# One conversion of the weights' low words: GpSimd in place of ScalarE

## The chip, the core and the metric

The program runs on one core of a Trainium2 chip. A core has five engines with a queue each: TensorE (PE for its matmuls, PEld for its weight loads), VectorE (DVE), ScalarE (ACT), GpSimd (POOL) and SyncE (SP), which here only issues DMAs. The metric is the device time of one execution in microseconds; lower is better.

## What is computed

Attention in a window for 8 batches and 8 heads (512 local and 32 global tokens, head size 64), followed by a feed-forward block over the 4352 resulting rows:

```python
s_ll = np.where(np.abs(pos[:, None] - pos[None, :]) <= 32, scale * q_l @ k_l.T, -1e9)
a_l = sm(np.concatenate([scale * q_l @ k_g.T, s_ll], axis=-1))
out_l = a_l @ np.concatenate([v_g, v_l])
out_g = sm(scale * q_g @ k_all.T) @ v_all
x = concat([out_g, out_l]) as rows of 512
h = x @ w_in                       # 512 x 2048
g = s * np.maximum(h, 0) ** 2 + b
out = g @ w_out                    # 2048 x 512
```

The two weight matrices come as float64. The kernel gets them as pairs of 32-bit words, a low word and a high word of each number, and makes float32 values of them on the chip.

## The kernel before

The attention is cut into 128 slots (`NS`), one for a batch, a half of its local tokens and a head. The feed-forward block works on 17 tiles of 256 rows, with 8 steps (`m`) of two 128-wide pieces of the hidden size each. One loop over `j` emits slot `j` of the attention, step `m = j - 10` of the feed-forward block, and the second product of the step before. In the first 16 slots the attention is computed on plain float32 operands (`scores32`, `transposes32`, `pv32`); from slot 16 on each operand is split into a rounded part and a rest (ScalarE rounds, GpSimd or VectorE subtracts: `split`, `v_split`, `g_load`). Between slots 0 and 9 blocks of four dummy matmuls (`keep_busy`) stand in TensorE's queue.

In those first 16 slots the weights are decoded too, one chunk of 128 hidden values in each: `weight_load` brings 512 KB of `w_in` and 512 KB of `w_out` into a staging tile `wst` (four buffers, whose places serve other tiles later), and `weight_words` decodes it in two halves of 128 x 512 numbers. So there are 32 halves. The six operations on a half, all in the functions printed below:

- line 160: the low words, every second word of `wst`, times 2^-29 as unsigned numbers, rounded into the integer tile `wup`. There are two places for `wup`, used in turn, so the one of a half can be written when the sum of line 165 two halves earlier has been read from it;
- line 161 (ScalarE): the high words as float, scaled, written over the low words of `wst`, thus only when line 160 has read them;
- line 164 (VectorE): those shifted left by three, in place;
- line 165 (VectorE): plus `wup`, an integer sum of two tiles in SBUF;
- line 168 (ScalarE): the rounded part into `w_all`;
- line 169 (VectorE): the rest into `w_all`. After this the staging buffer is free for the next load.

Each feed-forward step reads its two chunks of `w_all`, so the first tile of 256 rows can't be finished before the last chunk is decoded. The order of the instructions on each engine is set when the program is built, by a scheduler that plans with its own estimate of times; the loop's order and priorities enter it. Within an engine the instructions then run in that order.

Of the kernel before, what the change touches and what calls it, by code (L numbers as in the profile page):

```python
# [14 lines left out]
U32 = mybir.dt.uint32  # L15
U16 = mybir.dt.uint16
I16 = mybir.dt.int16
AF = mybir.ActivationFunctionType
ALU = mybir.AluOpType
# [46 lines left out]
def f32(ap):  # L66
    return ap.bitcast(F32)
# [3 lines left out]
def window_attention_then_ffn(ctx: ExitStack, tc: tile.TileContext, qd, qg, kw, vw, vg, qz, qgz, vz, w_in, w_out, sv, bv, out):  # L71
    nc = tc.nc
    scale = 1.0 / math.sqrt(D)
# [36 lines left out]
    for tile_, c0, shift in ((mask_low, 32, -32), (mask_mid, 32, 0), (mask_high, 0, 32)):  # L110
        nc.gpsimd.memset(tile_, 0.0)
        part = tile_[:, c0:c0 + 192]
        for sign, base in ((1, -shift), (-1, 64 + shift)):
            nc.gpsimd.affine_select(
                out=part, in_=part, pattern=[[sign, 192]], compare_op=ALU.is_ge,
# [31 lines left out]
    def weight_chunk(k):  # L147
        st = staged.pop(k)
        n = 2 if k < BY_HALVES else 1
        for i in range(n):  # L150
            c = 1024 // n
            weight_words(k, st[:, 2 * c * i:2 * c * (i + 1)], slice(c * i, c * (i + 1)))

    def weight_words(k, st, at):
        words = st.rearrange("p (n w) -> p n w", w=2)
        low, high = words[:, :, 0], words[:, :, 1]
        n = at.stop - at.start
        pool, tag = ((ops, "vsg"), (sb, "pg"))[(k + at.start // 512) % 2]
        up = pool.tile([P, n], I32, tag=tag, name=f"wup{k}_{at.start}", bufs=1)
        nc.scalar.activation(out=up, in_=low.bitcast(U32), func=AF.Copy, scale=2.0**-29)  # L160
        nc.scalar.activation(  # L161
            out=low.bitcast(F32), in_=high.bitcast(F32), func=AF.Prelu, scale=2.0**-112, alpha=2.0**32,
        )
        nc.vector.tensor_scalar(out=low, in0=low, scalar1=3, scalar2=None, op0=ALU.logical_shift_left)
        nc.vector.tensor_tensor(out=low, in0=low, in1=up, op=ALU.add)
        m = low.bitcast(F32)
        hi, lo = (w_all[:, i, k].rearrange("p w c -> p (w c)")[:, at] for i in range(2))
        nc.scalar.copy(out=hi, in_=m)  # L168
        nc.vector.tensor_sub(out=lo, in0=m, in1=f32(hi))  # L169
# [558 lines left out]
```

## Time and profile before

| | us |
|---|---|
| median of 3 runs (1012.46 to 1013.19) | 1012.96 |
| span of the profiled execution, first to last instruction | 1007.8 |
| TensorE matmul busy in the span | 993.5 |
| VectorE busy | 808.7 |
| ScalarE busy | 706.3 |
| GpSimd busy | 291.1 |

The median stands 5.2 us above the span of the profiled execution. Busy time of TensorE's matmuls runs to a modelled end, so the weight loads (904.7 us, 90% of the span) tell better where it stands still. All times in a trace are counted from the span's start.

### The profile page before, as it was taken

How to read it: one execution, taken by the hardware profiler on the slowest of the kernel's cores; microseconds unless marked ns; L12 is line 12 of the kernel's file. 1: busy time of each engine (PE TensorE's matmuls, PEld its weight loads, DVE VectorE, ACT ScalarE, POOL GpSimd, SP SyncE). 2: the span in 40 equal slices, each digit the busy share in tenths (PEclk: the TensorE clock that was granted, in tenths of full speed). 3: DMA queues.
4: the chain of work that ended last, by engine and by line, in shares of the span. 5: the costliest groups of instructions: out<-in, count | busy, mean ns of one | idle time of the engine just before them, and what ended most of it. 6: DMA issues, size and time to landing. Idle time of an engine off the chain costs nothing.

```text
span 1007.8 us, 20062 instructions
## 1 busy us (share of the span) xinstructions
PE 993.5 (99%) x6940; PEld 904.7 (90%) x6942; DVE 808.7 (80%) x2113; ACT 706.3 (70%) x1817; POOL 291.1 (29%) x366
## 2 busy tenths in 40 slices
PE   9899999999999999999999999999999999999998
PEld 5698899999999999999999999999999999999887
DVE  7999878978899779978799778988789788964322
ACT  8999867767677667858677667858677667743222
POOL 1001524323343233424243224424234223401000
PEclk9999999999999999999999999999999999999999
DMA  8765312213132212313122212313132112101000
GB/s 333 275 222 183 106 52 76 82 30 101 49 96 58 69 49 65 101 34 99 46 90 68 65 49 62 103 36 89 44 103 70 54 55 65 62 1 49 23 22 22
DMA packets 63845, 82.05 MB, mean 81 GB/s; under 512 B 7680, under 2 KB 51200, under 8 KB 63744
## 3 DMA queue, kind: packets, MB, share of 16 engines
q1 hardware_dynamic: 63168, 79.46, 25.4%
q10 hardware_dynamic: 576, 1.31, 0.4%
q8 instruction: 55, 0.90, 0.4%
q14 instruction: 46, 0.38, 0.1%
HBM read 71.30 MB, written 9.44 MB: 80 GB/s over the span
## 4 chain that ended last, share of the span: by engine, by line
PE 89%; ACT 7%; DVE 2%; DMA 1%; issue 0%; ACTq 0%; SPq 0%
PE ps_h L517 35%; PE acc L549 35%; PE ps_s L375 5%; PE ps_o L403 4%; PE turned L311 2%; PE turned L313 2%; PE ps_og L469 2%; ACT wst L161 1%; ACT w_all L168 1%; ACT wup L160 1%; PE ps_g L382 1%; ACT sm L231 1%; DMA wst<-in_w_out 1%; PE turned L447 1%; ACT pt L328 0%; DVE w_all L169 0%
## 5 line engine op out<-in xcount | busy, mean ns | idle before, releaser
L517 PE MATMUL ps_h<-xst,w_all 128*128 128x256 f32 x3264 | 437.0, 281 | 1.9 <-ACT xst L502 0.7
L549 PE MATMUL acc<-w_all,g 128*128 128x512 f32 x1632 | 421.5, 396 | 0.0
L517 PEld LDWEIGHTS ps_h<-xst,w_all 128*128 128x128 f32 x3264 | 406.9, 189 | 9.7 <-ACT xst L502 0.9
L549 PEld LDWEIGHTS acc<-w_all,g 128*128 128x128 f32 x1632 | 289.6, 188 | 49.7
L214 POOL TENSOR_TENSOR vs<-rv,vs 128x192 fp32r<-128x192 f32 x112 | 69.9, 624 | 313.3 <-ACT vs L213 312.2
L524 DVE SCALAR_TENSOR_TENSOR r<-ps_h,s_t,r 128x512 f32<-128x512 f32 x136 | 101.5, 746 | 52.4 <-ACT r L523 50.7
L231 ACT ACTIVATE sm<-sm,nm 128x224 f32<-128x224 f32 x256 | 121.7, 478 | 28.9 <-DVE nm L225 27.8
L532 DVE SCALAR_TENSOR_TENSOR g<-r,b_t,g 128x512 fp32r<-128x512 f32 x136 | 110.8, 815 | 35.6 <-ACT g L531 31.3
L531 ACT ACTIVATE g<-r,b_t 128x512 fp32r<-128x512 f32 x136 | 98.7, 725 | 52.2 <-DVE r L524 52.1
L206 POOL TENSOR_TENSOR kq<-rq,kq 128x256 fp32r<-128x256 f32 x112 | 94.5, 844 | 140.7 <-ACT kq L205 128.7
L523 ACT ACTIVATE r<-ps_h 128x512 f32<-128x512 f32 x136 | 81.3, 598 | 69.1 <-PE ps_h L517 58.1
L241 DVE TENSOR_SCALAR sm<-sm,nm 128x224 f32<-128x224 f32 x256 | 91.6, 399 | 3.9
L461 POOL TENSOR_TENSOR vsg<-rvg,vsg 128x320 fp32r<-128x320 f32 x64 | 57.1, 913 | 111.2 <-ACT vsg L460 111.2
L375 PE MATMUL ps_s<-kq 128*128 128x224 f32 x448 | 73.9, 275 | 1.9 <-DVE nm L225 1.9
L375 PEld LDWEIGHTS ps_s<-kq 128*128 128x128 f32 x448 | 67.2, 190 | 8.6 <-ACT kq L205 1.4
L392 ACT CAST pt<-turned 128x416 fp32r<-128x416 f32 x112 | 57.5, 513 | 24.8 <-PE turned L313 24.1
L393 DVE TENSOR_TENSOR pt<-turned,pt 128x416 fp32r<-128x416 f32 x112 | 65.5, 585 | 6.7 <-ACT pt L392 6.0
L386 ACT COPY tg<-ps_g 32x256 f32<-32x256 f32 (+1 forms) x112 | 42.1, 376 | 34.9 <-PE ps_g L382 32.5
L311 PE MATMUL turned<-ident,sm 128*96 128x128 f32 (+1 forms) x256 | 63.7, 273 | 1.2 <-ACT pt L328 1.0
L387 DVE TENSOR_TENSOR sg<-ps_g,tg 32x256 f32<-32x256 f32 (+1 forms) x112 | 48.2, 430 | 20.4 <-ACT tg L386 15.9
L204 POOL TENSOR_TENSOR kq<-rk,kq 64x352 fp32r<-64x352 f32 x56 | 61.7, 1102 | 4.4
L313 PE MATMUL turned<-ident,sm 128*128 128x128 f32 x256 | 62.8, 272 | 0.0
(81 smaller groups left out, 1288.7 us busy)
## 6 DMA issues: line engine op xcount, KB each, us to landing
rq<-in_qd SPq DMA_DIRECT2D x112, 128.0 KB, 2.1
rk<-in_kw SPq DMA_DIRECT2D x64, 176.0 KB, 2.3
rv<-in_vw SPq DMA_DIRECT2D x112, 96.0 KB, 1.9
rvg<-in_vg SPq DMA_DIRECT2D x32, 320.0 KB, 3.0
out<-o SPq DMA_DIRECT2D x32, 256.0 KB, 2.3
wst<-in_w_in SPq DMA_DIRECT2D x15, 512.0 KB, 4.6
wst<-in_w_out SPq DMA_DIRECT2D x15, 512.0 KB, 5.4
rv<-in_vz SPq DMA_DIRECT2D x16, 192.0 KB, 3.1
```

The source lines that it names most:

```text
L206: nc.gpsimd.tensor_sub(out=qs[:, 1, :], in0=rq, in1=f32(qs[:, 0, :]))
L231: nc.scalar.activation(out=p, in_=p, func=AF.Exp, bias=nm[:, blk:blk + 1], scale=-1.0, accum_out=ss[:, blk:blk + 1],)
L241: nc.vector.tensor_scalar(out=p, in0=p, scalar1=ss[:, blk:blk + 1], scalar2=1.0, op0=ALU.mult, op1=ALU.mult,)
L311: nc.tensor.transpose(out=p_t[0:n, s0:s0 + P], in_=sm[:, c0:c0 + n], identity=ident)
L313: nc.tensor.transpose(out=p_t[:, o0:o0 + P], in_=sm[:, c0:c0 + P], identity=ident)
L375: nc.tensor.matmul(p_s[:, W * blk:W * blk + W], lhsT=qs[:, a, blk * P:(blk + 1) * P], rhs=ks[:, KEYS[blk]], start=(a == 0), stop=(a == 1),)
L517: nc.tensor.matmul(p_h[:, k], lhsT=wi[:, a, f, c], rhs=xs[:, e, c, :], start=(n == 0), stop=(n == 11),)
L523: nc.scalar.activation(out=r, in_=p_h, func=AF.Relu)
L524: nc.vector.scalar_tensor_tensor(out=r, in0=p_h, scalar=s_t, in1=r, op0=ALU.mult, op1=ALU.mult)
L531: nc.scalar.activation(out=g[:, 0], in_=r, func=AF.Identity, bias=b_t)
L532: nc.vector.scalar_tensor_tensor(out=g[:, 1], in0=r, scalar=b_t, in1=f32(g[:, 0]), op0=ALU.add, op1=ALU.subtract,)
L549: nc.tensor.matmul(oacc[t][i], lhsT=g[:, a, k, i * P:(i + 1) * P], rhs=wo[:, e, f, :], start=(pr == 0 and n == 0), stop=(pr == 7 and n == 5),)
```

## The change

Line 160 is the only one that changes. The product with 2^-29 and the conversion from unsigned words to integers is issued to GpSimd as a tensor-scalar multiplication, no longer to ScalarE as an activation. Operands, tiles and buffers stay.

```diff
-        nc.scalar.activation(out=up, in_=low.bitcast(U32), func=AF.Copy, scale=2.0**-29)
+        nc.gpsimd.tensor_scalar(out=up, in0=low.bitcast(U32), scalar1=2.0**-29, scalar2=None, op0=ALU.mult)
```

The scheduler orders the program anew. On ScalarE the 32 instructions of line 160 leave the queue. At the second chunk (`wst_148`), before the change:

```order
L160 ACTIVATE wup_0_194<-wst_148 128x512
L300 COPY sg_176<-ps_g_313 64x256
L161 ACTIVATE wst_148<-wst_148 128x512
L160 ACTIVATE wup_512_201<-wst_148 128x512
L161 ACTIVATE wst_148<-wst_148 128x512
L328 COPY pt_233<-turned 128x416
L168 CAST w_all<-wst_148 128x512
```

and with it:

```order
L161 ACTIVATE wst_148<-wst_148 128x512
L328 COPY pt_233<-turned 128x416
L161 ACTIVATE wst_148<-wst_148 128x512
L168 CAST w_all<-wst_148 128x512
L231 ACTIVATE sm_315,nm_316<-sm_315,nm_316 128x224
L328 COPY pt_330<-turned 128x416
L231 ACTIVATE sm_315,nm_316<-sm_315,nm_316 128x224
L168 CAST w_all<-wst_148 128x512
```

Each line 161 now follows an instruction of another engine, where it followed one of its own queue.

On GpSimd the 32 instructions stand behind the making of the masks; most of them run where the queue held nothing, and the last ones among the first splits of queries, keys and values (`kq`, `vs`). The end of that stretch, as a difference (+ is with the change):

```order
+L160 TENSOR_SCALAR wup_512_919<-wst_729 128x512
 L214 TENSOR_TENSOR vs_1353<-rv_1198,vs_1353 128x3x64
+L160 TENSOR_SCALAR wup_0_912<-wst_729 128x512
+L160 TENSOR_SCALAR wup_0_1012<-wst_827 128x512
+L214 TENSOR_TENSOR vs_1475<-rv_1293,vs_1475 128x3x64
+L160 TENSOR_SCALAR wup_512_1019<-wst_827 128x512
+L160 TENSOR_SCALAR wup_512_1105<-wst_909 128x512
 L206 TENSOR_TENSOR kq_1091<-rq_1010,kq_1091 128x256
 L204 TENSOR_TENSOR kq_1091<-rk_1008,kq_1091 64x352
 L206 TENSOR_TENSOR kq_1091<-rq_1096,kq_1091 128x256
-L214 TENSOR_TENSOR vs_1475<-rv_1293,vs_1475 128x3x64
+L160 TENSOR_SCALAR wup_0_1098<-wst_909 128x512
```

All but the last conversion now stand ahead of the splits for slot 16 (`kq_1091`).

VectorE has the same instructions, in a somewhat other order. At the fourth chunk (`wst_191`), before the change:

```order
L164 TENSOR_SCALAR wst_191<-wst_191 128x512
L165 ISA wst_191<-wst_191,wup_0_291 128x512x2
L234 TENSOR_SCALAR nm_373<-nm_373 128x2
L164 TENSOR_SCALAR wst_191<-wst_191 128x512
L235 RECIPROCAL nm_373<-nm_373 128x2
L225 ISA sm_418,nm_419<-ps_s_413,mask_low 128x224
L225 ISA nm_419 128x1
L225 ISA sm_418,nm_419<-ps_s_413,mask_mid 128x224
L225 ISA nm_419 128x1
L165 ISA wst_191<-wst_191,wup_512_298 128x512x2
L241 TENSOR_SCALAR sm_372<-sm_372,nm_373 128x224 x2
```

and with it:

```order
L169 TENSOR_TENSOR w_all<-wst_151,w_all 128x512
L241 TENSOR_SCALAR sm_372<-sm_372,nm_373 128x224 x2
L169 TENSOR_TENSOR w_all<-wst_151,w_all 128x512
L234 TENSOR_SCALAR nm_419<-nm_419 128x2
L164 TENSOR_SCALAR wst_191<-wst_191 128x512
L235 RECIPROCAL nm_419<-nm_419 128x2
L165 ISA wst_191<-wst_191,wup_512_298 128x512x2
L241 TENSOR_SCALAR sm_418<-sm_418,nm_419 128x224 x2
L164 TENSOR_SCALAR wst_191<-wst_191 128x512
```

The softmax of the next slot (`sm_418`, `nm_419`) has moved ahead of the fourth chunk; what comes right behind line 165, whose end lets the next conversion into its `wup` tile, is in both orders mostly an instruction on tiles in SBUF (lines 234, 241, 164, 169).

## Rows read from the trace of the kernel before

**Rows 1.** The page: busy tenths in 40 equal slices of the span.

```profile
DVE  7999878978899779978799778988789788964322
ACT  8999867767677667858677667858677667743222
```

**Rows 2.** Busy by stretch: length, then PE, PEld, DVE, ACT, POOL (instructions), clock, DMA.

```profile
6.20:103.30 97.10, 90.90 (x563) 74.33 (x564) 92.60 (x265) 94.73 (x221) 7.03 (x8) 1.00 0.70 247
...
10.00:50.00 40.00, 35.21 (x201) 25.02 (x202) 37.76 (x132) 39.82 (x100) 0.00 (x0) 1.00 0.85 308
50.00:90.00 40.00, 40.00 (x274) 36.73 (x273) 38.15 (x99) 39.66 (x87) 1.03 (x1) 1.00 0.69 237
90.00:110.00 20.00, 17.37 (x111) 15.14 (x110) 18.49 (x45) 18.57 (x45) 10.02 (x12) 1.00 0.28 84
110.00:900.00 790.00, 790.00 (x5650) 731.51 (x5649) 674.46 (x1776) 569.83 (x1518) 271.57 (x333) 1.00 0.23 67
```

**Rows 3.** Chain of waits, 4 to 104 us: shares, and one piece (start, us, what).

```profile
by line: ACT wst L161 14.3%; ACT w_all L168 14.3%; ACT wup L160 14.1%; ACT sm L231 13.1%; DMA wst<-in_w_out 10.6%; ACT pt L328 4.4%; DVE w_all L169 3.9%; DVE wst L165 3.8%; DVE wst L164 2.7%; ACT g L531 2.5%; ACT r L523 2.4%; issue 2.2%; AC
...
22.89 0.57 ACT wup L160
```

**Rows 4.** Groups, 4.8 or 6.2 to 103.3 us: count | busy us, mean ns | idle before.

```profile
L160 ACT ACTIVATE wup<-wst 128x512 int32<-128x512 uint32 x32 | 22.2, 692 | 2.6 <-DMA wst<-in_w_in 2.2 <-DMA wst<-in_w_out 0.4
L161 ACT ACTIVATE wst<-wst 128x512 f32<-128x512 f32 x32 | 21.8, 685 | 0.2
...
L169 DVE TENSOR_TENSOR w_all<-wst,w_all 128x512 fp32r<-128x512 f32 x32 | 23.1, 723 | 0.8 <-ACT w_all L168 0.4
L165 DVE CUSTOM_DVE_ANT_0 wst<-wst,wup 128x1024 uint16<-128x1024 uint16 x32 | 22.4, 701 | 0.2
L164 DVE TENSOR_SCALAR wst<-wst 128x512 int32<-128x512 int32 x32 | 13.6, 424 | 7.0 <-ACT wst L161 6.7
```

**Rows 5.** Timeline of VectorE near 27 us: start, us, what.

```profile
26.59 0.69 DVE L165 CUSTOM_DVE_ANT_0 wst<-wst,wup 128x1024 uint16<-128x1024 uint16 x1
...
27.68 0.68 DVE L169 TENSOR_TENSOR w_all<-wst,w_all 128x512 fp32r<-128x512 f32 x1
```

**Rows 6.** Timeline of GpSimd, then of VectorE, 92 to 97 us.

```profile
92.30 0.96 POOL L206 TENSOR_TENSOR kq<-rq,kq 128x256 fp32r<-128x256 f32 x1
93.33 1.28 POOL L204 TENSOR_TENSOR kq<-rk,kq 64x352 fp32r<-64x352 f32 x1
94.69 1.07 POOL L206 TENSOR_TENSOR kq<-rq,kq 128x256 fp32r<-128x256 f32 x1
96.21 0.59 POOL L214 TENSOR_TENSOR vs<-rv,vs 128x192 fp32r<-128x192 f32 x1 [0.45 <-ACT vs L213]
...
92.68 1.12 DVE L165 CUSTOM_DVE_ANT_0 wst<-wst,wup 128x1024 uint16<-128x1024 uint16 x1
93.75 1.42 DVE L169 TENSOR_TENSOR w_all<-wst,w_all 128x512 fp32r<-128x512 f32 x1
95.09 0.74 DVE L524 SCALAR_TENSOR_TENSOR r<-ps_h,s_t,r 128x512 f32<-128x512 f32 x1
...
96.37 0.98 DVE L169 TENSOR_TENSOR w_all<-wst,w_all 128x512 fp32r<-128x512 f32 x1
```

**Rows 7.** GpSimd's instructions by line and shape, whole span: count | busy us, mean ns.

```profile
L214 POOL TENSOR_TENSOR vs<-rv,vs 128x192 fp32r<-128x192 f32 x112 | 69.9, 624 | 313.3 <-ACT vs L213 312.2 <-PE ps_s L375 1.1
...
L461 POOL TENSOR_TENSOR vsg<-rvg,vsg 128x320 fp32r<-128x320 f32 x64 | 57.1, 913 | 111.2 <-ACT vsg L460 111.2
...
L114 POOL TENSOR_SCALAR_AFFINE_SELECT mask_low<-mask_low 128x192 bf16<-128x192 bf16 x2 | 0.7, 345 | 0.0
...
masks.py:199 POOL TENSOR_SCALAR_AFFINE_SELECT ident<-ident 128x128 f32<-128x128 f32 x1 | 0.3, 292 | 0.0
```

**Rows 8.** The key splits on GpSimd by tile: shortest, median, longest ns.

```profile
L206 POOL TENSOR_TENSOR kq<-rq,kq x112: 724/740/1309, 92.3 to 872.5; 128x256 fp32r<-128x256 f32 x112
...
L204 POOL TENSOR_TENSOR kq<-rk,kq x56: 937/1109/1283, 93.3 to 871.3; 64x352 fp32r<-64x352 f32 x56
```

## The prediction

> **What bounds the kernel now.** I read the 40 slices of the page first [rows 1]. The four slices of the first 100 us look unlike the rest: ScalarE and VectorE both stand at eight or nine tenths. All that the change touches lies there: the weights are decoded between 4.8 and 103.3 us [rows 4]. The table by stretch says what each part is worth [rows 2]. From 110 to 900 us TensorE's weight loads are busy 731.5 of 790 us (93%) and nothing else is full: that part is TensorE's own. From 10 to 50 us they are busy 25.0 of 40 us (63%), from 50 to 90 us 36.7 of 40 (92%, as later), and from 90 to 110 us 15.1 of 20 (76%). So TensorE loses time in the first 110 us, by waiting for the engines that decode weights and do the softmax. A microsecond that this head gains or loses moves the end by a microsecond, because the work that TensorE has behind the last decoded chunk stays the same.
>
> Which engine sets the head? The chain of waits runs along ScalarE: line 160 alone has 14.1% of the 100 us from 4 to 104 [rows 3]. In the stretch from VectorE's first decoding step to the end of its last one, 6.2 to 103.3 us, ScalarE is busy 94.7 of 97.1 us; but VectorE is busy 92.6 of the same 97.1 [rows 2]. It is idle for 4.5 us in all. This is the number on which the case turns: the chain names ScalarE, and VectorE stands 4.5 us behind it.
>
> **What the change takes away.** ScalarE loses 32 instructions. A piece of line 160 takes 0.57 us of the chain [rows 3] (its 692 ns of [rows 4] overlap the neighbours), so 32 x 0.57 = 18.2 us leave ScalarE's queue. ScalarE would then need 94.7 - 18.2 = 76.5 us of the 97.1. VectorE's own work is not shortened by it at all: it still has 92.6 us to do. What can be won is its idle time, 4.5 us, and not all of that: some is the gap between one engine's end and the next one's start, and some a staging load still under way. I let 1.5 us of it stay: gain 3.0 us, bounds 0 and 4.5.
>
> **What it adds.** 32 instructions on GpSimd, whose queue was empty for most of this time (7.0 us busy of 97.1 [rows 2]). Its own time is covered many times over. A conversion can start when line 165 two halves earlier has ended; halves come every 97.1 / 32 = 3.0 us, so 6.1 us are there for the conversion, line 161 (0.69), line 164 (0.42) and what they queue for. On ScalarE, line 161 now waits for GpSimd, with exponentials and roundings of other slots queued behind it; ScalarE has 18 us to spare for that. The loads of `wst` stay on their queue and still wait for line 169. All of this I cost at nothing, as long as a conversion takes under 3 us or so.
>
> What is not covered is what GpSimd does to VectorE. Near 27 us, with GpSimd idle, line 165 takes 0.69 us and line 169 0.68 [rows 5]. Between 92.3 and 96.8 us GpSimd works on four splits, and in that time line 165 takes 1.12, one line 169 takes 1.42 and another 0.98 [rows 6]. Line 524, one of whose operands is in PSUM, takes 0.74 in the same time, as it always does. So an instruction of VectorE on two tiles in SBUF stands still while GpSimd is at work. The loss there is 0.43 + 0.74 + 0.30 = 1.47 us for four instructions of GpSimd, 0.37 us for one. It is the same mix of work on VectorE as in the rest of the head: lines 164, 165 and 169 alone are 59 of its 92.6 us [rows 2, 4].
>
> These four were 256, 352, 256 and 192 elements long; taken at the medians for the first three and the mean for the fourth (740, 1109, 740, 624 ns [rows 7, 8]) one is about 0.80 us. The trace has no conversion on GpSimd, so I bound it. From above, by its two-operand rows: 624 ns for 192 elements and 913 for 320 are 2.26 ns per element, which makes 913 + 192 x 2.26 = 1.35 us for 512 [rows 7]. From below, by its rows with one operand: 292 ns for 128 and 345 for 192 are 0.83 ns per element, so 345 + 320 x 0.83 = 0.61 us [rows 7]. The conversion reads one tile, which puts it nearer to the lower end, but also converts at either side of the product, which the mask rows don't. I take 0.80 us. The loss per instruction is then that of the four, 0.37 us, and 32 x 0.37 = 11.8 us. At 0.61 us a wait is shorter by 0.19: 32 x 0.18 = 5.8 us. At 1.35 us it is longer by 0.55: 32 x 0.92 = 29.4 us. That a conversion costs VectorE nothing can't be excluded by these rows, since all four splits read two tiles; the lowest end is therefore 0.
>
> The Trainium skill has a rule on that last point. Its page "SBUF — State Buffer", section "Who interferes with whom", says that GpSimd and VectorE share a pair of ports under an exclusive lock, and that a VectorE instruction with two SBUF inputs, or in a mode that uses both ports, contends with any GpSimd instruction that reads SBUF. By it one operand is enough and the sum stands at 11.8 us; without it the lower end would be 0. The rows of two-operand splits agree with it (1.12 us against 0.69 for line 165); that a one-operand instruction does the same, no row here shows.
>
> **The sum.** VectorE in the head: 92.6 + 11.8 us of work and waits and 1.5 us idle, 105.9 us where there were 97.1. That is 8.8 us more, and VectorE takes ScalarE's place as the bound. The span of 1007.8 becomes 1016.6; with the 5.2 us that the median stands above the span, 1021.8 us. With 5.8 to 18 us of loss the same case gives some 1015 to 1029 us.
>
> **The rivals.**
> - *The chain's promise.* The head gives back what line 160 has on the chain, 14.1 us [rows 3]: 1012.96 - 14.1 = 998.9 us. Against it stand VectorE's 4.5 idle us: it would have to finish 92.6 us of work in 83. It would take a head in which VectorE's rows hold slack inside.
> - *No contention with one operand.* If the conversion leaves VectorE alone, the freed ScalarE gives the idle time back: 3.0 us, 1010.0 us, and 1008.5 at most. This one ends on the faster side; it decides as soon as the loss per conversion is under 3.0 / 32 = 0.09 us. For it: no row shows a one-operand instruction beside a slowed VectorE. Against: splits of every line are seen to do it.
> - *A short conversion.* GpSimd runs at the pace of its one-operand rows, 0.61 us: 5.8 us lost and 3.0 to 4.5 won, 1014.3 to 1015.8 us. The page "GPSIMD Engine Reference" of the Trainium skill, section "Engine selection", speaks for it: one-input operations there run at roughly line rate. The mask rows (0.83 ns per element) agree; whether a conversion from strided words does, none shows.
> - *A long conversion.* At the two-operand rate or slower, 29.4 us lost and 3.0 won: 1039.4 us. For it: reading every second word and converting twice may cost GpSimd as much as a second operand.
>
> **How the numbers follow.** Forecast (VectorE bound, 1021.8): 0.58. Short conversion: 0.13. No contention: 0.12. Long conversion: 0.13. The chain's promise: 0.04. The runs of before spread over 0.7 us, and about 0.2% (2 us) is what a measurement can tell from no change. Faster by more: the chain's promise and most of no contention and a little of the short conversion, 0.15. Within: more than half of the short conversion and the rest of no contention, 0.12. Slower: 0.73. For 8 times in 10 the range has to take in the forecast's own 1015 to 1029, the short conversion, a part of no contention, and some of the way to the long one: 1010 to 1034.
>
> **What would show it.** In the head of the changed kernel: lines 165, 169 and 164 longer than their 0.69, 0.68 and 0.42 us wherever a line 160 of GpSimd lies beside them, by about 0.37 us for each line 160; the last line 169 ending near 112 us, not 103.3; VectorE full and ScalarE at about 75 to 80% up to there; TensorE's losses all before 120 us, and the same 93% after it; the chain of waits in the head on VectorE and GpSimd. I am wrong in size if line 160 takes far from 0.80 us on GpSimd; wrong in the mechanism if lines 165 and 169 keep their length beside it, or if the head ends earlier than 103 us although VectorE works as long as before.

## The result

The changed kernel takes 1024.59 us (median of 1021.07 to 1026.19) where the kernel before takes 1012.71 in the same comparison: a ratio of 1.0121, 95% interval [1.0106, 1.0136]. That is slower by 11.9 us, on the side the prediction named and inside its range, 2.8 us above its 1021.8.

The profiled execution took 1024.31 us, its span is 1022.5. The profiled execution of before, with its span of 1007.8, was about 3 us quicker than its own median: in all kernels run here the time of a profiled execution stands 1.8 to 2.2 us above its span, so it took some 1010. Differences between the two traces (14.7 us in the span) are therefore about 3 us larger than that of the medians.

The 40 slices of the page, to be held against [rows 1]: the first four of ScalarE stand at 6 to 8 tenths, no longer 8 or 9, VectorE's stay as full as they were, and TensorE's granted clock, 1.00 in every slice before, dips in the fourth and fifth.

```profile
DVE  6999888898799788998789788988899788964322
ACT  6876676777678676777678676867678676844222
PEclk9998899999999999999999999999999999999999
```

The table by stretch, to be held against [rows 2]; the first row runs from VectorE's first decoding step to the end of its last one. Columns: stretch and length, then busy time (instructions) of PE, PEld, DVE, ACT and POOL, granted clock, share of the DMA engines, GB/s.

```profile
7.30:115.70 108.40, 94.74 (x550) 76.66 (x549) 103.78 (x265) 80.14 (x191) 61.02 (x39) 0.94 0.66 222
...
10.00:50.00 40.00, 35.53 (x201) 24.96 (x200) 39.57 (x128) 32.97 (x86) 20.60 (x13) 1.00 0.85 293
50.00:90.00 40.00, 37.78 (x253) 34.68 (x253) 38.74 (x94) 29.11 (x66) 22.49 (x13) 1.00 0.63 207
90.00:110.00 20.00, 13.03 (x70) 10.70 (x68) 17.99 (x28) 13.45 (x27) 15.02 (x12) 0.82 0.43 139
110.00:130.00 20.00, 19.35 (x119) 17.34 (x120) 15.82 (x41) 14.34 (x39) 8.58 (x10) 0.84 0.24 66
130.00:900.00 770.00, 769.17 (x5498) 711.59 (x5498) 658.48 (x1738) 557.88 (x1490) 266.68 (x329) 1.00 0.23 68
```

VectorE issues the same 265 instructions in the head as before, but needs 103.78 us for them instead of 92.60, and the head is 108.4 us long instead of 97.1. It is idle for 4.6 us of it, before 4.5. ScalarE fell from 98% busy to 74%. TensorE's weight loads lose nothing of their busy time up to 50 us (24.96 against 25.02), 2.0 us from 50 to 90, 4.4 us from 90 to 110 and 1.4 us from 110 to 130; behind 130 us they are busy 92% of the time, as before.

Busy time hides a part of this. The kernel before has from 110 to 130 us:

```profile
110.00:130.00 20.00, 20.00 (x155) 18.75 (x154) 18.58 (x44) 16.27 (x45) 10.70 (x12) 1.00 0.34 101
```

The changed kernel is about as busy there, but with 119 matmuls at a granted clock of 0.84 in place of 155 at 1.00. Counted in matmuls it falls behind by 0, 21, 41 and 36 in the four stretches from 10 to 130 us, by 98 in all. At the 0.14 us that one takes behind 130 us (770 us for 5498) these are some 13.7 of the 14.7 us; this is an estimate, since the matmuls differ in size.

The groups of VectorE for the same stretch (line, tiles, shapes, count, then busy us, mean ns, then idle time before), to be held against [rows 4], and GpSimd's from the page of the whole execution:

```profile
L169 DVE TENSOR_TENSOR w_all<-wst,w_all 128x512 fp32r<-128x512 f32 x32 | 26.2, 823 | 1.2 <-ACT w_all L168 0.9
L165 DVE CUSTOM_DVE_ANT_0 wst<-wst,wup 128x1024 uint16<-128x1024 uint16 x32 | 22.4, 700 | 1.0
L164 DVE TENSOR_SCALAR wst<-wst 128x512 int32<-128x512 int32 x32 | 16.0, 504 | 7.4 <-ACT wst L161 7.2
L241 DVE TENSOR_SCALAR sm<-sm,nm 128x224 f32<-128x224 f32 x34 | 14.1, 455 | 0.1
...
L234 DVE TENSOR_SCALAR nm<-nm 128x2 f32<-128x2 f32 x17 | 5.0, 292 | 0.2 <-ACT sm L231 0.2
...
L160 POOL TENSOR_SCALAR wup<-wst 128x512 int32<-128x512 uint32 x32 | 55.7, 1741 | 38.7 <-DVE wst L165 20.3
```

Two of VectorE's groups are not in the rows shown of before; in the head there (6.2 to 103.3 us) they read:

```profile
L241 DVE TENSOR_SCALAR sm<-sm,nm 128x224 f32<-128x224 f32 x34 | 9.9, 331 | 0.1
...
L234 DVE TENSOR_SCALAR nm<-nm 128x2 f32<-128x2 f32 x17 | 3.2, 189 | 0.3
```

So at equal counts line 169 costs 3.1 us more, line 241 4.2, line 164 2.4, line 234 1.8; line 165 keeps its length. A conversion takes 1741 ns on GpSimd in the mean. How the two engines meet is seen in the timelines of GpSimd and of VectorE (start, us, what):

```profile
82.49 1.70 POOL L160 TENSOR_SCALAR wup<-wst 128x512 int32<-128x512 uint32 x1 [2.33 <-DVE nm L235]
84.37 1.90 POOL L160 TENSOR_SCALAR wup<-wst 128x512 int32<-128x512 uint32 x1 [0.18 <-DVE wst L165]
87.85 1.96 POOL L160 TENSOR_SCALAR wup<-wst 128x512 int32<-128x512 uint32 x1 [1.58 <-DVE wst L165]
...
83.61 0.68 DVE L165 CUSTOM_DVE_ANT_0 wst<-wst,wup 128x1024 uint16<-128x1024 uint16 x1
84.21 1.73 DVE L169 TENSOR_TENSOR w_all<-wst,w_all 128x512 fp32r<-128x512 f32 x2
...
88.35 0.86 DVE L164 TENSOR_SCALAR wst<-wst 128x512 int32<-128x512 int32 x1
89.13 0.68 DVE L169 TENSOR_TENSOR w_all<-wst,w_all 128x512 fp32r<-128x512 f32 x1
...
114.96 0.69 DVE L169 TENSOR_TENSOR w_all<-wst,w_all 128x512 fp32r<-128x512 f32 x1
```

At 88.35 line 164 takes 0.86 us instead of 0.42, and the line 169 behind it, still beside the same conversion, its usual 0.68. VectorE loses 0.44 us to a conversion that lasts 1.96. At 83.61 line 165 lies beside a conversion and keeps its 0.68 us.

The trace shows the same over the whole head. The table counts, for each line, the instructions that lie beside no instruction of GpSimd, those that lie beside conversions alone, and how many of either are lengthened (over 0.1 us longer than the shortest of the line); the other three of lines 164, 165 and 169 each lie beside splits.

| line | beside nothing: lengthened | beside conversions alone: lengthened |
|---|---|---|
| 241 | 11: 0 | 23: 12 |
| 234 | 11: 0 | 6: 6 |
| 164 | 15: 0 | 14: 5 |
| 169 | 8: 0 | 21: 7 |
| 165 | 19: 0 | 10: 0 |

So none of these instructions grew where GpSimd stood still, and not every meeting costs. What decides which one does isn't shown. The last line 169 ends at 115.65 us.

### The profile page after: what moved, and what is told of

It reads as the page before. It is cut to its first block, busy times and chain, and to the rows that moved or that the text cites. A ratio compares the mean times of both kernels' runs of the same rounds, so it can differ in the third digit from the quotient of the medians.

```text
span 1022.5 us, 20162 instructions
## 1 busy us (share of the span) xinstructions
PE 1000.9 (98%) x6942; PEld 909.1 (89%) x6942; DVE 819.8 (80%) x2113; ACT 690.8 (68%) x1785; POOL 345.5 (34%) x398
## 4 chain that ended last, share of the span: by engine, by line
PE 78%; DVE 1%; ACT 1%; DMA 0%; issue 0%; DVEq 0%; ACTq 0%
PE acc L549 31%; PE ps_h L517 31%; PE ps_s L375 4%; PE ps_o L403 4%; PE turned L311 2%; PE turned L313 2%; PE ps_og L469 2%; PE ps_g L382 1%; PE turned L447 1%; ACT sm L231 0%; DMA rq<-in_qd 0%; ACT kq L203 0%; DVE r L524 0%; DVE sm L241 0%; PE turned L500 0%
## 5 line engine op out<-in xcount | busy, mean ns | idle before, releaser
L549 PE MATMUL acc<-w_all,g 128*128 128x512 f32 x1632 | 426.8, 399 | 3.0 <-ACT g L531 3.0
L241 DVE TENSOR_SCALAR sm<-sm,nm 128x224 f32<-128x224 f32 x256 | 94.9, 412 | 4.0
L160 POOL TENSOR_SCALAR wup<-wst 128x512 int32<-128x512 uint32 x32 | 55.7, 1741 | 38.7 <-DVE wst L165 20.3
L403 PE MATMUL ps_o<-pt,vs 128*128 128x256 f32 x336 | 62.9, 295 | 0.0
```

What stands on the lines that cost most here:

```text
L241: nc.vector.tensor_scalar(out=p, in0=p, scalar1=ss[:, blk:blk + 1], scalar2=1.0, op0=ALU.mult, op1=ALU.mult,)
L403: nc.tensor.matmul(p_o[:, :, q], lhsT=vs[0:n, c], rhs=pt[0:n, :, o], start=(c == 0), stop=(c == 1))
L549: nc.tensor.matmul(oacc[t][i], lhsT=g[:, a, k, i * P:(i + 1) * P], rhs=wo[:, e, f, :], start=(pr == 0 and n == 0), stop=(pr == 7 and n == 5),)
```

## The experiments

Two questions stood open. Is the loss VectorE's meeting with GpSimd, or the new waits on GpSimd? And what part of it is the order, which the scheduler makes anew for every edit?

**No conversion at all (e1).** L165 adds a tile of zeros, so the low words' part is left out.

```diff
-        nc.scalar.activation(out=up, in_=low.bitcast(U32), func=AF.Copy, scale=2.0**-29)
+        up = no_up[:, 0:n]
```

> The kernel before with line 160 left out: nobody converts the low words, and line 165 adds a tile of zeros that is written once (so the lowest three bits of the weights are missing). ScalarE loses its 32 conversions, GpSimd gets nothing. Theory of VectorE as the bound: what can be won is VectorE's idle time in the head, 0 to 4.5 us, so 1008 to 1013 us. Rival, the chain names the bound: the 14 us that line 160 has on the chain come off, about 999 us.

Measured: 1019.6 us, ratio 1.0076 [1.006, 1.0093]. Less work on ScalarE, nothing on GpSimd, and still 8 us slower: both theories failed. The profiled execution was the slowest of the four, 1023.66 us. What TensorE waited for (line, releaser: us, times, longest), two stretches, and the lines 169 (shortest, median, longest ns, then first and last start):

```profile
PE ps_g L295 <- DMA rk<-in_kw: 6.3, 2, 3.6
```

```profile
40.00:50.00 10.00, 5.97 (x23) 4.22 (x24) 9.24 (x31) 6.95 (x17) 0.00 (x0) 0.77 0.80 277
60.00:70.00 10.00, 6.95 (x31) 6.08 (x32) 8.32 (x20) 8.23 (x18) 0.54 (x1) 0.66 0.69 216
```

```profile
L169 DVE TENSOR_TENSOR w_all<-wst,w_all x32: 668/687/695, 8.4 to 97.5; 128x512 fp32r<-128x512 f32 x32
```

The last chunk is decoded at 98.2 us, 5 us earlier than before; the time was lost elsewhere. In the new order key loads came late, TensorE stood, and its clock fell between 40 and 70 us, where the kernel before has 1.00. An order can thus cost most of what the change costs (7.7 us here, 11.9 there), and no kernel that is planned anew tells the price of its edit alone.

**The conversion beside the kernel before (e2).** ScalarE keeps its conversion; GpSimd makes a second one that nobody reads.

```diff
+        nc.gpsimd.tensor_scalar(out=low, in0=low.bitcast(U32), scalar1=2.0**-29, scalar2=None, op0=ALU.mult)
```

> The kernel before, with line 160 on ScalarE as it was, and a second conversion of the same shape on GpSimd behind line 169, whose result nobody reads (it goes over the words of the staging tile, which are dead by then). Nothing waits for it but the next load into the staging tile. Theory of the port: VectorE stands still for some 0.35 us per conversion, lines 164, 169 and 241 grow by some 11 us in sum, and the time is 1020 to 1026 us although ScalarE works as before. Rival, the waits for GpSimd's result make the difference: 1012 to 1014 us.

Measured: 1022.35 us, ratio 1.0108 [1.0093, 1.0123]. Nobody waits for the result, and the loss is there. But it isn't clean: the tile it writes is the staging tile, and the next weight load waits for it. SyncE's queue (line, releaser: us, times, longest):

```profile
SPq L145 <- POOL wst L170: 23.1, 7, 5.8
```

**Both edits (e3).** No conversion on the path, an unread one on GpSimd, into a tile of its own.

```diff
-        nc.scalar.activation(out=up, in_=low.bitcast(U32), func=AF.Copy, scale=2.0**-29)
+        up = no_up[:, 0:n]
...
+        nc.gpsimd.tensor_scalar(out=beside[:, 0:n], in0=low.bitcast(U32), scalar1=2.0**-29, scalar2=None, op0=ALU.mult)
```

> Both of these at once: no conversion on ScalarE (line 165 adds a tile of zeros), and a conversion on GpSimd behind line 169 into a tile that nobody reads. It has the changed kernel's load on every engine, without its waits of ScalarE and VectorE for GpSimd. Theory of the port: as slow as the changed kernel, 1020 to 1025 us. Rival, the handover from GpSimd to ScalarE to VectorE is what costs: as fast as the kernel without any conversion, 1008 to 1013 us.

Measured: 1026.85 us, ratio 1.0155 [1.014, 1.017]; against e1, 7.3 us more. Up to the end of the last chunk VectorE is busy 96.6 us with 240 instructions (5.8 to 104.4 us), in e1 84.7 with 242 (5.6 to 98.2): again a loss that no wait on the conversion explains. But it is yet another order, with a granted clock of 0.50 from 50 to 60 us, so the 7.3 us aren't the price of the conversions alone.

**The conversion on VectorE (e4).**

```diff
-        nc.scalar.activation(out=up, in_=low.bitcast(U32), func=AF.Copy, scale=2.0**-29)
+        nc.vector.tensor_scalar(out=up, in0=low.bitcast(U32), scalar1=2.0**-29, scalar2=None, op0=ALU.mult)
```

> Line 160 on VectorE, as the same tensor-scalar multiplication. GpSimd stays idle in the head. Theory of VectorE as the bound: 32 instructions of 0.34 us (the pace of line 164) to 0.61 us (of line 169) are added to a full queue, 11 to 19 us, and at most 4.5 us of idle time is won: 1020 to 1031 us. Rival, the handovers cost: one queue less to hand over to, 1013 to 1016 us.

Measured: 1019.69 us, ratio 1.0081 [1.0066, 1.0096]: slower, as a full VectorE has it, by a little less than the 1020 us that went with it. VectorE's own conversions are cheap:

```profile
L160 DVE TENSOR_SCALAR wup<-wst 128x512 int32<-128x512 uint32 x32 | 13.9, 436 | 4.7 <-DMA wst<-in_w_in 3.7 <-DMA wst<-in_w_out 0.9
```

13.9 us of work, where GpSimd doing the same lengthened VectorE's other instructions by 11.2 us.

**A third place for the result (e5).** The changed kernel, with a third buffer for `up` in the first 12 chunks, so that GpSimd can run further ahead.

```diff
-        pool, tag = ((ops, "vsg"), (sb, "pg"))[(k + at.start // 512) % 2]
+        i2 = 2 * k + at.start // 512
+        pool, tag = ((ops, "vsg"), (sb, "pg"), (sb, "rvg"))[i2 % 3 if k < 12 else i2 % 2]
```

> The changed kernel with a third place for the converted words in the first twelve chunks (a tile that stands empty until slot 16), so that GpSimd's conversion waits for line 165 three halves earlier, not two. Theory of the port: VectorE is full in the head, an earlier conversion changes nothing, 1022 to 1026 us. Rival, GpSimd comes too late: it waited 20 us for line 165 in sum, and the time falls by 4 us or more, to 1020 us or less.

Measured: 1018.44 us, ratio 1.0074 [1.0058, 1.0091], some 5 us better than the change and in the range of the rival. The last chunk's rest (line 170 in this program) and TensorE from 40 to 50 us:

```profile
L170 DVE TENSOR_TENSOR w_all<-wst,w_all x32: 664/678/1166, 11.2 to 104.8; 128x512 fp32r<-128x512 f32 x32
```

```profile
40.00:50.00 10.00, 8.55 (x36) 6.43 (x36) 10.00 (x30) 7.40 (x18) 5.79 (x5) 0.71 0.58 185
```

The decoding ends at 105.5 us, 10 us earlier than in the changed kernel, with VectorE idle for 0.7 us of it and no longer 4.6. The first theory, by which an earlier conversion changes nothing, missed this. The time gained is only half of that, since TensorE now loses earlier, at a granted clock of 0.71. Either the waits for a place or the order could be the reason for the earlier end; this run can't tell.

**The meeting measured by itself (e6).** The kernel before with a section behind its end: GpSimd's operations alone, then eight subtractions of two tiles on VectorE alone and beside three instructions of GpSimd, then one-operand multiplications beside three conversions.

```diff
+    for _ in range(12):
+        nc.vector.tensor_scalar(out=g1[:, 0:512], in0=near, scalar1=2.0, scalar2=1.0, op0=ALU.mult, op1=ALU.mult)
+    convert(3)
...
+    subs(8)
+    for _ in range(3):
+        nc.gpsimd.memset(g0, 0.0)
```

> The kernel before with work added behind its end, where all engines are idle, so its time says nothing. First the conversion alone on GpSimd, in five kinds (float or integer words in and out, next to each other or every second one): the time of one. Then eight VectorE subtractions of 128 x 512 alone, and the same beside three conversions, beside three GpSimd subtractions, beside three GpSimd fills, and beside three float multiplications; and twelve one-operand VectorE multiplications beside three conversions. Theory that a conversion keeps the port for its whole 1.5 us: VectorE loses 1.3 us for each, 3.9 us in sum. Theory that it keeps it only while it reads: 0.3 to 0.5 us for each, 0.9 to 1.5 us in sum. If the integer types make the conversion long, the float multiplication takes about 0.6 us; if every second word does, the one on neighbouring words.

It took 1069.92 us with that section. GpSimd's groups: the plain product from float to float and the conversion between contiguous words, alone; the subtraction and the memset, beside VectorE's rows.

```profile
L666 POOL TENSOR_SCALAR m_pool<-m_src 128x512 f32<-128x512 f32 x2 | 3.0, 1492 | 47.8 <-PE acc L549 47.7
...
L666 POOL TENSOR_SCALAR m_pool<-m_src 128x512 int32<-128x512 uint32 x2 | 3.0, 1487 | 0.2
...
L703 POOL TENSOR_TENSOR m_pool<-m_src 128x512 f32<-128x512 f32 x3 | 4.9, 1645 | 0.2
...
L707 POOL MEMSET m_pool<- 128x1024 f32 x3 | 2.9, 951 | 0.2
```

The conversion itself is free there: any product of 512 elements takes 1.49 us. VectorE's groups, in order: two operands alone; beside conversions; one operand beside conversions; one operand alone; two operands beside subtractions.

```profile
L674 DVE TENSOR_TENSOR m_dve<-m_src 128x512 f32<-128x512 f32 x8 | 5.5, 692 | 0.5 <-POOL m_pool L678 0.3
...
L674 DVE TENSOR_TENSOR m_dve<-m_src 128x512 f32<-128x512 f32 x8 | 6.5, 809 | 0.6 <-POOL m_pool L678 0.3
...
L698 DVE TENSOR_SCALAR m_dve<-m_src 128x512 f32<-128x512 f32 x7 | 5.2, 737 | 0.5 <-POOL m_pool L678 0.3
...
L698 DVE TENSOR_SCALAR m_dve<-m_src 128x512 f32<-128x512 f32 x5 | 2.1, 427 | 0.2
...
L674 DVE TENSOR_TENSOR m_dve<-m_src 128x512 f32<-128x512 f32 x8 | 8.4, 1045 | 0.5 <-POOL m_pool L678 0.3
```

A conversion costs a row of two-operand subtractions (809 - 692) x 8 / 3 = 0.31 us, and a row of one-operand multiplications (737 - 427) x 7 / 3 = 0.72 us. A two-operand instruction of GpSimd takes no longer there than a conversion (1.65 us, against 1.79 beside the same row), but costs (1045 - 692) x 8 / 3 = 0.94 us. Beside three memsets the two-operand group reads 692 ns, as alone; beside three products from float to float 800, or 0.29 us for one. So the price of a meeting goes by which two instructions meet, not by GpSimd's length alone. GpSimd loses too: beside VectorE's two rows a conversion takes 1.79 and 1.62 us in the mean, not 1.49.

**The order held.** For the other six runs the order was no longer left to the scheduler: TensorE's, VectorE's, ScalarE's and SyncE's instructions each got an edge, of order alone, to the one that stands ahead of it in another kernel's program. That the order was held shows in the traces: the first 900 instructions of TensorE, VectorE and ScalarE (line 160 apart) stand in the same order before and in e7, e8, e9 and e11. The kernel before wasn't run with such edges in its own order.

```diff
+            if ahead is not None:
+                tc.add_manual_dep(
+                    i, ahead.name,
+                    mybir.DependencyInfo(mybir.DependencyClass.NoSync, mybir.DependencyReason.DATA),
+                    reason="order",
+                )
+            ahead = i
```

The change in the order of before (e7):

> The changed kernel with the instructions of TensorE, VectorE, ScalarE and SyncE held in the order of the kernel before, one behind the other (only the 32 conversions leave ScalarE's row; GpSimd's own order stays the scheduler's). If GpSimd's conversions at VectorE's cost are the loss, nothing is won back by it: 1021 to 1026 us, last L169 at 113 to 117 us. If the new order that the scheduler made is a good part of it, 1015 to 1019 us. If VectorE now waits for a conversion that comes late in a fixed order, above 1026.

Measured: 1019.31 us, ratio 1.0081 [1.0064, 1.0098], just above the range that went with the order. Its head, as a stretch and in two groups:

```profile
7.30:112.70 105.40, 91.91 (x547) 74.80 (x548) 100.54 (x265) 80.73 (x190) 60.45 (x39) 0.97 0.65 225
```

```profile
L169 DVE TENSOR_TENSOR w_all<-wst,w_all 128x512 fp32r<-128x512 f32 x32 | 23.0, 719 | 0.4 <-ACT w_all L168 0.3
...
L164 DVE TENSOR_SCALAR wst<-wst 128x512 int32<-128x512 int32 x32 | 17.2, 542 | 8.2 <-ACT wst L161 8.1
```

VectorE is busy 7.9 us longer than before, idle 4.9 us, and the time is 8.2 us longer. Line 164 suffers more than in the changed kernel (542 ns against 504), line 169 not at all (719 ns; 723 before): which instruction is lengthened is a matter of the order.

The unread conversion in the order of before (e8), with the same line added as in e2:

> The kernel before with the unread conversion on GpSimd behind each L169, and the order of the four other engines held as before. Nothing but GpSimd's access to memory can cost here: with the loss of VectorE alone (32 times 0.3 to 0.4 us, all on the path) 1020 to 1024 us; if the planner's new order was the larger part of the 10.5 us of the unheld version, 1013 to 1017 us.

Measured: 1025.91 us, ratio 1.0143 [1.0128, 1.0158], above both. VectorE's head and SyncE's queue:

```profile
6.40:114.90 108.50, 94.18 (x560) 75.90 (x561) 102.42 (x265) 96.29 (x220) 60.67 (x37) 0.97 0.63 221
```

```profile
SPq L145 <- POOL wst L170: 31.8, 11, 5.4
```

VectorE is busy 9.8 us longer; on top of that the weight loads waited 31.8 us in all for the unread conversion. The edit added a wait that the change does not have, so e2 and e8 set no price of the meeting alone.

No conversion in the order of before (e9), edited as e1:

> No conversion on any engine (L165 adds a zero tile), in the order of the kernel before. If VectorE bounds the head and ScalarE's relief is worth only VectorE's idle time: 1008 to 1013 us. If the unheld version without conversions was slow because weight loads that start earlier push the key loads back, in any order: 1015 to 1021 us.

Measured: 1009.71 us, ratio 0.9986 [0.9977, 0.9996].

```profile
5.70:103.00 97.30, 90.40 (x552) 74.75 (x553) 90.61 (x265) 79.99 (x189) 7.01 (x8) 0.98 0.72 250
```

This is all that ScalarE's relief is worth: 1.4 us, with no conversion anywhere. The head is as long as before (97.3 us), VectorE's idle time in it grew to 6.7. Against e1, the same work in another order, it is some 9 us less (0.9986 against 1.0076). The idea that weight loads freed earlier push the key loads back in any order falls with it.

This is also the run to hold e7 against. In one order, e7 has the conversions on GpSimd and the waits for them, and e9 has neither: VectorE is busy 9.9 us longer in e7, idle 1.8 us less, and the time is 9.6 us longer. The loss lies in VectorE's longer instructions; no waiting of VectorE is added.

The kernel before in the order of the changed one (e10):

> The kernel before (conversion on ScalarE) with the four engines held in the order that the scheduler made for the changed kernel. No conversion runs on GpSimd, so what is lost here is the order's own price. If the loss is GpSimd's access: 1011 to 1014 us. If the order is a good part of it: 1016 to 1021 us, with TensorE's granted clock below 1.00 somewhere between 40 and 120 us.

ScalarE's own line 160, which has no place in that order, was left to the scheduler.

Measured: 1019.15 us, ratio 1.0079 [1.0064, 1.0094].

```profile
6.40:111.90 105.50, 93.76 (x556) 76.58 (x555) 93.45 (x265) 96.18 (x221) 6.91 (x8) 0.97 0.68 231
```

VectorE is hardly busier than before (93.45 us) but idle for 12.1: the scheduler made that order for a ScalarE without line 160, and with it there VectorE waits. So the order has a price, but this one is not what it costs the changed kernel.

**Memsets in place of the conversion.** GpSimd's work at L160 waits for the same, is waited for by the same and lasts about 2.0 us ((11.3 for the columns + 53.5 for the memsets) / 32), but hardly reads; `up` is left zero.

```diff
-        nc.gpsimd.tensor_scalar(out=up, in0=low.bitcast(U32), scalar1=2.0**-29, scalar2=None, op0=ALU.mult)
+        nc.gpsimd.tensor_scalar(out=up[:, 0:1], in0=low[:, 0:1].bitcast(U32), scalar1=2.0**-29, scalar2=None, op0=ALU.mult)
+        for _ in range(3):
+            nc.gpsimd.memset(up, 0)
```

In the order of before (e11), and in the changed kernel's (e12):

> As the changed kernel in the order of before (1019.3 us), but GpSimd's work at L160 is one converted column and three memsets of the same tile, together about as long (3 times 0.48 us and the column) and waiting for the same things and waited for by the same L165; the other columns' low words are left out. In the micro-measurement a memset did not lengthen VectorE's instructions. If the loss is access to memory: 1009 to 1012 us, with L164 back at 0.42 us. If the loss is the later place in GpSimd's row and the waits on it: 1016 to 1021 us.

> The same memsets in place of the conversion, in the order that the scheduler made for the changed kernel (1022.4 to 1024.6 us). If access to memory is the whole loss there too: 1010 to 1013 us. If that order has a price of its own beside it: 1014 to 1018 us. If waits or order are all of it: 1020 or more.

Measured: e11 1017.1 us, ratio 1.0053 [1.0041, 1.0065], in the range that went with the waits; e12 1021.91 us, ratio 1.0107 [1.0094, 1.0121], where waits or order were to be all of it. Head and groups of e11 (its lines 166, 171 and 243 are 164, 169 and 241 elsewhere), then the head of e12:

```profile
6.00:109.00 103.00, 92.61 (x561) 75.76 (x562) 97.78 (x265) 81.18 (x191) 71.06 (x134) 0.98 0.69 235
```

```profile
L171 DVE TENSOR_TENSOR w_all<-wst,w_all 128x512 fp32r<-128x512 f32 x32 | 21.8, 681 | 0.6 <-ACT w_all L170 0.6
L166 DVE TENSOR_SCALAR wst<-wst 128x512 int32<-128x512 int32 x32 | 17.1, 537 | 4.9 <-ACT wst L163 4.9
L243 DVE TENSOR_SCALAR sm<-sm,nm 128x224 f32<-128x224 f32 x34 | 14.7, 469 | 0.1
```

```profile
6.00:113.60 107.60, 95.78 (x557) 77.57 (x556) 100.20 (x265) 80.30 (x189) 71.83 (x134) 0.95 0.67 228
```

I had taken memsets for harmless, from two-operand neighbours alone. The one-operand lines 164 and 241 are lengthened beside them as beside conversions (537 and 469 ns); the two-operand line 169 keeps its 0.68 us. By overlap in the trace, of the instructions beside memsets alone 9 of 14 of the first and 12 of 13 of the second are lengthened in e11, none of 17 of line 169 and none of 12 of line 165. So e11's time doesn't tell the waits from the meetings. VectorE's head is 5.2 us busier in e11 and 7.6 in e12. So these runs took away a part of the meetings, not all, and the price of the waits alone stays unmeasured.

## Why the prediction came out as it did

- **The bound.** Right. VectorE stood right behind ScalarE, and it sets the head of the changed kernel: busy 103.78 of 108.4 us, while ScalarE has 28 us to spare (it was relieved of 94.73 - 80.14 = 14.6 us, not of 18.2). The chain's promise of 14.1 us was never there: without any conversion, in the same order, 1.4 us are won (e9).
- **A microsecond of the head is one of the time.** Right where the order was held, with one exception: heads 0.2, 5.9, 8.3, 8.4 and 10.5 us longer than before (e9, e11, e7, e10, e12) go with times -1.4, +5.6, +8.2, +8.1 and +10.5 us; e8, with 11.4 and +14.8, has a second stretch of a lower clock (0.83 from 120 to 130 us). Wrong as a rule: in e1, e3 and e5 the last chunk is decoded at 98.2, 104.4 and 105.5 us (103.3 before), and the times are 7.7, 15.0 and 7.4 us longer, since TensorE lost its time earlier, at granted clocks down to 0.66, 0.50 and 0.71.
- **The gain of 3.0 us.** Mis-sized. In the changed kernel VectorE is idle for 4.6 us, as before, so nothing was won; with no conversion at all e9 wins 1.4 us, and there the head is no shorter in the trace.
- **The length of a conversion.** Mis-sized. 0.80 us was taken, 1.35 the upper bound; it is 1.49 alone (e6) and 1.74 in the mean here, beside VectorE's work. I scaled by the mask rows and the splits [rows 7, 8]; a product on 512 elements has neither's pace. The Trainium skill, in "GPSIMD Engine Reference", section "Engine selection", puts one-input work at roughly line rate; the 1492 ns of the plain product against VectorE's 427 for one of the same shape do not agree.
- **The loss of 0.37 us for one.** Right in size, by luck: two errors cancel. The added busy time is 103.78 - 92.60 = 11.2 us, 0.35 for each conversion, beside the 11.8 forecast. But the rule that a longer conversion holds VectorE longer by as much was wrong: at 1.35 us it gave 0.92 us each and 29.4 in all, and at 1.74 the loss is 0.35. By overlap in the trace, of the 32 conversions 6 lengthen nothing, 16 one instruction of VectorE, 9 two and 1 three, by 0.14 to 0.53 us each; the rest pass. And the 11.2 us hold for this order alone: in the order of before they are 7.9 (e7).
- **Which instructions.** Right that one operand on GpSimd's side is enough, and that lines 164 and 169 lengthen; wrong on line 165, which keeps its 700 ns. Ten of its 32 lie beside conversions alone and none of them is lengthened; the two that are (0.86 and 1.01 us) lie beside splits, as did the 1.12 us of [rows 6] from which the prediction took it. That isn't fixed either: in e2 conversions lengthen 5 of 23. Line 241 and the small line 234, which the prediction didn't name, carry 6.0 us.
- **The waits costed at nothing.** About right. ScalarE's line 161 waits 6.9 us in all for GpSimd, and ScalarE has that to spare; VectorE's idle time did not grow.
- **The order.** The step that is missing. The sum moved the 32 conversions and left all else in place. In that setting the sum was close, +8.8 forecast and 8.2 us measured (e7), but by luck: its parts are 7.9 us of work and no gain, where 11.8 and 3.0 were forecast. The scheduler's own order adds some 3.7 us (1.0121 against 1.0081, intervals that don't overlap): with the same 265 instructions in the head VectorE is busy 103.78 us in it and 100.54 in the order of before, mostly since conversions lengthen 7 lines 169 there and 2 in e7, though 21 and 17 lie beside them.
- **The added 5.2 us** from the span to the median. Wrong as a constant: it is 1.8 us for the changed kernel's profiled execution. The trace of before was a quick execution. (By the sum's own terms 5.8 to 18 us of loss give 1015.8 to 1028.0 us, not 1015 to 1029.)
- **Where TensorE loses.** Right on the side of 120 us. Not foreseen is that it loses in lumps: nothing up to 50 us, and most between 90 and 130 (77 of the 98 matmuls), where the last chunks come late and the granted clock falls. The chain in the head could not be followed in the trace of after, so the forecast that it runs on VectorE and GpSimd stays untested.

What TensorE waited for from 5 to 130 us in the changed kernel (line, releaser: us, times, longest), the last pieces of the weights and the `g` made from their products:

```profile
PE acc L549 <- ACT g L531: 3.0, 1, 3.0
...
PE ps_h L517 <- DVE w_all L169: 2.0, 2, 1.1
PE ps_h L517 <- ACT w_all L168: 1.9, 1, 1.9
```

## What to carry to other kernels

Work taken off one of two engines that are both full is worth at most the other's idle time; look for that first. GpSimd is not free ground for it: 32 products on GpSimd took 11.2 us of VectorE, nearly the 13.9 that VectorE needs to make them itself. And where a scheduler orders the program, a new order can move the time as much as the edit: hold the order before pricing an edit, and price an order with the work unchanged.

## What the runs showed of the hardware

- GpSimd needs 1.49 us for a product on 128x512 words, whether it converts or not and whether the words are contiguous or not (1487 to 1508 ns alone in e6), 1.65 for a subtraction of two tiles beside VectorE, and 0.95 for a memset of twice the size.
- VectorE's delay depends on the pair. Two operands on VectorE: 0.31 us for a one-operand product on GpSimd, 0.94 for a subtraction, none for a memset. One operand on VectorE: 0.72 us for a product, and a delay beside memsets too (line 164: 537 ns in e11, 424 before). These are means of rows in e6; in the kernel many meetings pass without a delay. The Trainium skill says the same of the pairs ("SBUF — State Buffer", "Who interferes with whom"): a two-input instruction of VectorE contends with a GpSimd instruction that reads, not with one that only writes, and a one-input instruction in a mode that takes both ports contends with either. It also says that the loser is blocked for the other's whole instruction; the trace does not agree, with 0.44 us lost beside a conversion of 1.96, and with ten lines 165, of two operands, not lengthened at all in the changed kernel. Whether lines 164 and 241 run in such a mode, no run here shows.
- In the changed kernel and in e1, TensorE's granted clock fell where the engine had stood for want of weights or keys: 0.82 from 90 to 110 us in the one, 0.66 from 60 to 70 us in the other, each a mean over stretches at its two levels, 1.2 and 2.4 GHz. A fall is not a loss by itself: e9 has 0.98 over its head and is the quickest kernel here. What part of the change's 11.9 us is the clock's was not separated.
